# A linear-attention prologue in front of a squared-ReLU feed-forward: one weight load issued earlier, one product on another engine, two input loads swapped

## The chip, the cores and the metric

The kernel runs on one core of one Trainium2 chip. The metric is device time in microseconds (us) of one execution; lower is better. The core has a matrix engine (PE, TensorE), three engines for elementwise work (DVE = VectorE, ACT = ScalarE, POOL = GpSimd), a queue engine (SP, SyncE) that here only issues DMAs, and 16 DMA engines which all queues share. DMAs issued by SP and ACT show in the profile as hardware queues (q1 for SP, q10 for ACT), those issued by POOL as the software queue q0.

## The reference

Two stages, in fp32. The first is a recurrent linear attention over 4 batches, 8 heads, 768 steps and head size 48; the second is a feed-forward layer with a squared ReLU on its output.

```python
for t in range(S):                                            # r, k, v: [B, H, S, D]; w, u: [H, D]
    cur = einsum('bhd,bhe->bhde', u * k[:, :, t], v[:, :, t])
    y[:, :, t] = einsum('bhd,bhde->bhe', r[:, :, t], state + cur)
    state = w[..., None] * state + einsum('bhd,bhe->bhde', k[:, :, t], v[:, :, t])
x = y.transpose(0, 2, 1, 3).reshape(B * S, H * D)             # 3072 x 384
h = maximum(x @ w_in, 0)                                      # w_in: 384 x 2048
out = (h * h) @ w_out                                         # w_out: 2048 x 384
```

## The kernel before, in words

The 768 steps of a batch are cut into 6 chunks of 128, so there are 24 **units** (batch, chunk). Within a unit the recurrence becomes matrix products: keys and receptances are scaled by powers of w (`kh`, `rh`), transposed on PE (`T`, and for the first units `TK`, `TR`), multiplied with each other (`A`), masked (`Bm`), and multiplied with v (`Y`); the state goes from one unit of a batch to the next through a product k·v (`U`, in pairs `UP`) and elementwise updates (`S0`, `ts`, `S`). The term with u is a row sum: `P0` = r·k, `P1` = P0·u, `du` = sum over the head, `dv` = v·du. The result of a unit is copied out of PSUM (`xs`), transposed (`X`, then `xTc`), multiplied with W1 = w_in (`F1`, and `FA` for parts of the first group), passed through ReLU and square (`re`, `sq`), multiplied with W2 = w_out (`F2`), copied (`os`) and stored (`out`).

Units 0 to 3 are handled as two **pairs**: pair 0 is units 0 and 1 (the first two chunks of batch 0), pair 1 is units 2 and 3 (those of batch 1). One load `lp.x.q` brings r, k or v of pair q as 384 KB, in 128 partitions with 8 pieces of 384 bytes each, that is 1024 DMA packets. Later units are loaded one by one (`ld`, 192 KB, pieces of 192 bytes). `Ap.q`, `Bp.q`, `YE.q` / `YD.q`, `YI` and `UP.q` are the pair's forms of A, Bm, Y and U. W1 is loaded in four quarters `V.0` to `V.3` of 512 columns each, W2 in four quarters `W.0` to `W.3`, all by POOL with a cast to bf16; a W1 quarter is 128 partitions with 3 pieces of 1024 bytes, 384 packets. `FA` needs quarter 3, then `F1` of the first group needs quarters 0, 1 and 2. `Z.n` is n tiles of dummy products with the identity.

Nothing is scheduled at run time. A table `ORDER`, read from left to right, gives every step with its engine (A, D, G = POOL, P = PE, S = SP) and, behind the slashes, the buffer or PSUM bank it takes; each engine runs its own steps in this order and waits on semaphores for the others. `UP.1:P/7/3` is the state product of pair 1 on PE into banks 7 and 3. In the trace a step is found by its line: L332 the pair loads, L328 the single loads, L338 V, L341 W, L344 kh, L347 rh, L350 P0, L354 P1, L357 du, L362 dv, L371 TR and TK, L391 Ap, L399 Bp, L456 and L465 YE, L435 and L444 YD, L475 YI, L498 UP, L522 S0, L525 ts, L533 X, L561 FA, L549 F1, L589 F2. Copies by ACT or DVE have the lines of a helper (L257 and L259) and are told apart by their tiles: `rkT` is a copy of transposed keys or receptances (`RC`, `KC`), `vb` the bf16 copy of v, `xs` and `xT` those of the results. In the order's rows the tiles carry numbers: `P_82` belongs to unit 1 and `P_83` to unit 0, `ldv_71` and `ldv_72` hold v of pairs 0 and 1, `ldk_67` and `ldk_68` k of pairs 0 and 1, `W_0` to `W_3` with numbers 183 to 186 are the W1 quarters.

In the table before, the first steps of SP are r.0, k.0, r.1, v.0, k.1, v.1 (pairs 0 and 1) and then single loads of units 4 and 5; POOL makes masks (`mP`, `mJ`), then P0 of unit 1, three W1 quarters, P1 of unit 0, the last W1 quarter and dv of units 1 and 0.

Of the kernel before, what the change touches and what calls it, by code (L numbers as in the profile page):

```python
# [24 lines left out]
ORDER = """
w:A mP.0:G mP.1:G lp.r.0:S/0 lp.k.0:S/0 tab:A lw:A Z.8:P/0 u:A w4:A bw:P/1 lp.r.1:S/1 lp.v.0:S/0 mJ:G lp.k.1:S/1
bu:P/6 Wt.1:A/2 lp.v.1:S/1 Wt.0:A/5 rh.1:D/0 P0.1:G/0 Wk.0:A/4 rh.0:D/1 Wk.1:A/7 ld.r.5:S/4 kh.0:D/1 V.3:G kh.1:D/0
ub:A l4:A TR.0:P/0 P0.0:D/1 V.0:G ld.k.4:S/4 RC.0:A/0 TK.0:P/3 rh.3:D/2 rh.2:D/3 V.1:G P1.1:D du.1:D/1 bc:P/6 TR.1:P/2
KC.0:A/1 ld.r.4:S/5 P1.0:G WLcol:A vb.0:A/0 vb.1:A/1 kh.2:D/3 kh.3:D/2 Z.2:P/5 Ap.0.1:P/0/3 Ap.0.0:P/4/6 V.2:G
TK.1:P/5 ld.k.5:S/5 dv.1:G du.0:D/0 dv.0:G RC.1:A/2 WLm:A Bp.0.1.1:D/0 UP.0:P/7/3 Bp.0.0.1:D/2 YE.0.1:P/2/6  # L30
Bp.0.1.0:D/1 KC.1:A/3 vb.3:A/2 Z.7:P/0 vb.2:A/3 Bp.0.0.0:D/3 YE.0.0:P/2/6 Ap.1.0:P/5/4 P0.2:G/2 S0.0:D ld.v.4:S/4
P1.2:G ts.1:D/1 xs.0:A/0 YI.1:P X.0:P/0 Bp.1.0.1:D/4 UP.1:P/7/3 xs.1:A/1 xTc.0:D/3 Bp.1.0.0:D/6 S0.2:D X.1:P/2
FA.0.0:P/6/4 ts.3:D/0 xTc.1:A/3 FA.0.1:P/6/4 P0.3:G/3 P1.3:G du.2:D/2 F1.0.0:P/5 dv.2:G du.3:D/3 dv.3:G W.2:G Wt.2:A
re.0.6:A/0 re.0.0:A/1 ld.v.5:S/5 Wk.2:A W.1:G rh.5:G/4 W.3:G W.0:G F1.0.1:P/2 Ap.1.1:P/0/6 Bp.1.1.1:D/5 F1.0.2:P/7
re.0.1:A/2 F1.0.3:P/5 re.0.7:A/3 Bp.1.1.0:D/7 YD.1:P/1/2 YI.3:P sq.0.7:A/0 re.0.3:A/4 xs.3:D/2 xs.2:A/3 kh.4:D/5
re.0.2:A/5 ld.k.6:S/6 F1.0.4:P/6 X.2:P/4 X.3:P/2 xTc.3:A/0 sq.0.0:A/2 xTc.2:D/0 sq.0.1:A/1 rh.4:D/5 F1.0.5:P/5
re.0.4:D/3 sq.0.6:A/3 re.0.5:A/2 P0.4:D/4 F1.1.4:P/1 T.4:P/0 Tc.4:D/4 F1.1.7:P/4 sq.0.5:D/4 F1.1.5:P/3 re.1.4:D/1
re.1.7:A/0 ld.r.6:S/6 sq.0.4:A/5 F1.1.1:P/0 re.1.5:D/2 re.1.1:A/3 sq.1.5:D/6 sq.0.3:D/7 F1.1.0:P/6 kh.5:D/4 F1.1.2:P/4
sq.1.1:A/8 F1.1.6:P/5 re.1.2:A/2 re.1.0:D/4 T.5:P/0 re.1.6:D/3 F2.0.2:P/4 F1.1.3:P/6 ld.r.7:S/7 Tc.5:A/5 sq.0.2:D/9
P1.4:D du.4:D/4 A.4:P/5/0 A.5:P/1/2 sq.1.6:A/10 re.1.3:A/5 sq.1.3:A/11 F2.0.1:P/4 sq.1.0:A/12 F2.0.3:P/4 vb.4:G/4  # L40
Bm.4.1:D/0 Bm.4.0:D/1 sq.1.7:A/13 P0.5:D/1 Bm.5.1:D/2 sq.1.4:A/14 F2.1.1:P/5 Bm.5.0:D/3 F2.1.2:P/5 ld.k.7:S/7 dv.4:G
F2.3.2:P/6 Y.4:P/0 P1.5:G sq.1.2:A/15 ld.v.7:S/6 ld.k.9:S/0 xs.4:D/4 du.5:D/0 F2.0.0:P/4 vb.5:A/5 F2.3.0:P/6 Y.5:P/0
dv.5:D xs.5:D/0 P0.6:G/0 P1.6:G ld.v.6:S/7 F2.3.1:P/6 os.0:D/0 ld.r.9:S/0 X.4:P/3 xTc.4:D/1 U.4:P/7 F2.1.0:P/5 X.5:P/0
F2.1.3:P/5 xTc.5:D/1 rh.7:G/6 F1.2.0:P/4 os.1:D/1 S0.4:D F1.2.4:P/0 P0.7:G/2 re.2.0:D/3 out.1:S F1.2.2:P/5 kh.7:D/6
re.2.4:A/5 kh.6:G/0 F1.2.6:P/4 re.2.6:A/4 ld.r.8:S/1 vb.6:A/6 re.2.2:A/0 XB.7:S/6 rh.6:D/0 F1.2.3:P/0 F2.3.3:P/6
kh.9:D/1 re.2.3:A/1 P1.7:D XB.6:S/1 F2.2.2:P/4 du.7:D/1 os.3:D/2 F1.2.1:P/5 S.1:D ld.k.8:S/1 U.5:P/0 S0.5:D dv.7:G
# [9 lines left out]
A.9:P/6/4 A.11:P/1/2 P0.11:D/2 P1.11:G sq.3.2:A/27 F2.6.0:P/3 ld.r.12:S/4 Bm.9.1:D/2 re.3.5:A/3 F2.6.1:P/3 A.8:P/4/0
sq.3.7:A/5 Bm.9.0:D/3 ld.v.12:S/4 dv.9:G sq.3.5:A/7 Bm.11.1:D/5 F1.3.6:P/5 Bm.11.0:D/7 sq.3.4:A/3 du.8:D/4 re.3.6:A/5
F2.7.0:P/2 Bm.8.0:D/0 sq.3.6:A/9 ld.k.12:S/5 ld.r.15:S/7 Y.9:P/1 vb.11:A/2 F2.7.2:P/2 Bm.8.1:D/1 dv.8:D S.9:G
vb.10:A/3 ld.k.14:S/7 F2.6.3:P/3 out.4:A P1.10:G Y.8:P/4 xs.9:D/3 F2.7.3:P/2 A.10:P/5/7 U.10:P/0 xs.8:D/4 P0.13:G/0
kh.13:G/4 X.9:P/6 Bm.10.1:D/4 X.8:P/1 F2.6.2:P/3 xTc.8:A/0 xTc.9:D/0 du.11:D/0 rh.12:G/0 Y.11:P/4 du.10:D/2 dv.10:G  # L60
# [42 lines left out]
re.10.5:D/5 Y.23:P/4 sq.10.5:D/22 F2.19.2:P/6 xs.23:D/3 re.10.3:A/4 sq.10.3:A/23 xX.23:S/1 sq.10.2:A/0 F1.10.6:P/4
F1.10.4:P/0 F2.21.1:P/5 F1.11.1:P/3 out.17:G F1.11.0:P/1 out.16:G re.11.1:D/1 re.11.0:A/0 re.10.1:A/5 sq.11.0:D/27
re.10.4:D/4 F1.11.3:P/2 sq.10.1:D/1 sq.10.4:A/6 re.11.3:D/3 F1.11.2:P/3 sq.11.3:D/3 F2.20.1:P/1 F1.12.1:P/7
re.11.2:A/0 F1.12.2:P/0 F1.12.0:P/2 F2.19.3:P/6 sq.10.0:D/26 re.12.2:D/5 sq.12.2:A/24 re.12.1:D/4 F2.21.2:P/5
sq.11.2:A/25 F1.10.7:P/3 re.10.6:A/3 F2.22.2:P/0 sq.10.6:A/4 re.10.7:D/2 re.12.0:A/5 F2.20.2:P/1 sq.11.1:D/5
sq.10.7:D/10 sq.12.0:A/14 F1.12.3:P/7 sq.12.1:D/18 F2.20.3:P/1 re.12.3:A/0 F2.20.0:P/1 Fh.23.2.0:P/4 os.20:A/5
# [585 lines left out]
```

## Time and profile before

| | |
|---|---|
| times of three runs | 169.10, 171.58, 173.42 us; median 171.58 us |
| profiled execution | 168.49 us, of which its span is 166.8 us |
| busy share of the span | PE 97%, DVE 80%, ACT 62%, POOL 60% |
| DMA moved in the span | 28.02 MB, mean 168 GB/s |
| granted PE clock | full in all 40 slices |

The profiled execution is 3.1 us below the median of the runs and 0.6 us below the lowest. Its span starts with the first instruction; 1.7 us of its time lie outside of it. The page has each engine's busy share; the views on which the prediction draws are the chain of work that ended last (each step followed back to what released it), the timeline by engine (start, duration, engine, line, output<-input, number of instructions merged into the row, and in brackets the idle time before it with its releaser) and the DMA view of a window (packets, MB and busy share by queue; for the DMAs issued in the window their size and the time from issue to landing).

### The profile page before, as it was taken

The page shows a single profiled execution, that of the slowest core. Times are in us where ns is not written, and L with a number is a line of the kernel's source. Part 1 is how long each engine was busy: PE and PEld are TensorE (multiplying, and loading weights), DVE is VectorE, ACT ScalarE, POOL GpSimd, SP SyncE. Part 2 cuts the span into 40 slices and gives each one's busy share as a digit, 9 for nine tenths or more (in the row PEclk, how much of TensorE's full clock was granted, in tenths as well). Part 3 has the DMA queues.
Part 4 walks back from the last instruction along what each step waited for, and adds up shares of the span by engine and source line. Part 5 has one row for each costly group of instructions (what it writes and reads, how often), then busy time and mean ns, then how long its engine had stood idle before and what let it go on. Part 6 is the DMA issues. An engine that isn't in the chain of part 4 may idle for free.

```text
span 166.8 us, 4505 instructions
## 1 busy us (share of the span) xinstructions
...
## 2 busy tenths in 40 slices
...
GB/s 131 324 240 193 201 179 196 196 211 175 157 208 211 176 193 222 171 207 169 216 186 75 221 223 176 216 213 180 193 145 174 192 97 21 120 73 0 2 145 95
DMA packets 97713, 28.02 MB, mean 168 GB/s; under 512 B 92538, under 2 KB 97404, under 8 KB 97692
## 3 DMA queue, kind: packets, MB, share of 16 engines
...
q0 software_dynamic: 3072, 4.33, 13.3%
...
q14 instruction: 7, 0.06, 0.1%
...
## 4 chain that ended last, share of the span: by engine, by line
PE 95%; DMA 2%; ACT 1%; ACTq 0%; issue 0%
PE bank L549 37%; PE bank L589 37%; PE bank L418 4%; PE bank L488 2%; PE bank L371 2%; DMA urow<-in_u_dram 2%; PE bank L486 2%; PE bank L508 2%; PE bank L533 2%; PE bank L603 2%; PE bank L278 1%; PE bank L561 1%; PE bank L391 1%; PE bank L498 1%; PE bank L405 1%; ACT L269 0%
## 5 line engine op out<-in xcount | busy, mean ns | idle before, releaser
L589 PE MATMUL bank<-W,hq 128*128 128x384 bf16 x368 | 68.7, 326 | 0.0
L549 PE MATMUL bank<-xT,W 128*128 128x256 bf16 (+1 forms) x612 | 68.1, 264 | 0.0
L571 ACT ACTIVATE hr<-bank 128x512 bf16<-128x512 f32 x69 | 40.1, 594 | 35.3 <-PE bank L549 33.0
L549 PEld LDWEIGHTS <-W 128*128 128x128 bf16 x612 | 55.0, 98 | 8.4 <-issue 0.6
L589 PEld LDWEIGHTS <-hq 128*128 128x128 bf16 x368 | 33.5, 98 | 18.5
L578 ACT ACTIVATE hq<-hr 128x512 bf16<-128x512 bf16 x72 | 41.9, 625 | 6.0 <-DVE hr L573 5.4
L426 DVE TENSOR_TENSOR Bm<-bank,maskJT 128x512 bf16<-128x512 f32 x40 | 25.5, 681 | 3.7 <-PE bank L418 3.7
L573 DVE TENSOR_SCALAR hr<-bank 128x512 bf16<-128x512 f32 x27 | 18.1, 681 | 5.6 <-PE bank L549 4.0
L354 POOL TENSOR_TENSOR P<-P,ub 128x384 f32<-128x384 f32 x15 | 16.7, 1111 | 6.0 <-DVE P L350 5.4
L362 POOL TENSOR_TENSOR dv<-ldv,du 128x384 f32<-128x384 f32 (+1 forms) x18 | 15.1, 849 | 6.9 <-DVE du L357 4.4
L347 POOL TENSOR_TENSOR rk<-ldr,Wt 128x384 bf16<-128x384 f32 x15 | 15.8, 1056 | 0.0
L350 POOL TENSOR_TENSOR P<-ldr,ldk 128x384 f32<-128x384 f32 x13 | 13.6, 1046 | 3.0 <-DMA ldr<-in_r_dram 1.8
L519 DVE TENSOR_TENSOR xs<-bank,dv 128x384 bf16<-128x384 f32 x20 | 11.0, 552 | 4.4 <-PE bank L488 2.1
L528 POOL TENSOR_TENSOR S0W<-ts,WLm 128x384 bf16<-128x384 f32 x10 | 11.0, 1104 | 4.7 <-DVE ts L525 3.3
L580 DVE TENSOR_TENSOR hq<-hr 128x512 bf16<-128x512 bf16 x24 | 12.9, 550 | 1.2 <-ACT hr L571 0.8
L259 POOL CAST vb<-ldv 128x384 bf16<-128x384 f32 x10 | 5.6, 557 | 13.1 <-DMA ldv<-in_v_dram 13.1
L344 POOL TENSOR_TENSOR rk<-ldk,Wk 128x384 bf16<-128x384 f32 x12 | 12.6, 1056 | 1.2 <-DMA ldk<-in_k_dram 1.2
L357 DVE TENSOR_REDUCE du<-P 128x8 f32<-128x384 f32 x24 | 12.9, 542 | 0.3 <-POOL P L354 0.2
L259 DVE COPY os<-bank 128x384 f32<-128x384 f32 x11 | 6.0, 549 | 6.2 <-PE bank L589 6.1
L525 DVE TENSOR_TENSOR ts<-bank,S0W 128x384 f32<-128x384 f32 x16 | 8.8, 547 | 2.7 <-PE bank L508 2.5
L488 PE MATMUL bank<-vb,Bm 128*128 128x48 bf16 x160 | 9.5, 183 | 0.0
L257 ACT COPY xT<-bank 128x384 bf16<-128x384 bf16 x8 | 3.7, 480 | 8.5 <-PE bank L533 8.5
...
## 6 DMA issues: line engine op xcount, KB each, us to landing
...
W<-in_moe_w_in_dram POOLq DMA_DIRECT2D x4, 384.0 KB, 9.0
W<-in_moe_w_out_dram POOLq DMA_DIRECT2D x4, 384.0 KB, 7.8
...
```

The costliest lines, as they stand in the source:

```text
L347: e.tensor_mul(rk[slot[f"rk{i}"]][:, 0, :, 0:D], loaded("r", i), Do.factor("t", i % 2 if i < PAIRED else 2))
L350: e.tensor_mul(P0b[slot[f"P{i}"]], loaded("r", i), loaded("k", i))
L354: e.tensor_mul(t, t, bank("bu")[:, 0 : H * D].rearrange("p (h d) -> p h d", h=H) if i in EARLY_U else ub)
L357: e.tensor_reduce(dub[slot[f"dv{i}"]], P0b[slot[f"P{i}"]], axis=mybir.AxisListType.X, op=ALU.add)
L362: e.tensor_mul(dv_of(i) if i < PAIRED else dvb[slot[f"dv{i}"]], loaded("v", i), t)
L426: e.tensor_mul(Bmb[slot[f"Bm{i}{h}"]], heads(bank(f"bA{i}{h}"), 128), mask_b)
L549: e.matmul(hp[:, fi, :], W1[f // 4][:, c, 256 * (f // 2 % 2) : 256 * (f // 2 % 2 + 1)].rearrange("p (m j) -> p j m", j=2)[:, f % 2, :], xt ...
L571: e.activation(hr, hp, AF.Relu)
L573: e.tensor_scalar_max(hr, hp, 0.0)
L578: e.activation(hq, hr, AF.Square)
L580: e.tensor_mul(hq, hr, hr)
L589: e.matmul(bank(f"bO{i}")[:, 0:d_model], hqb[slot[f"hq{g},{f // m}"]][:, at : at + L], W2[q][:, f % 4, :], start=(seen[i] == 1 and f % 4 = ...
```

## The change

Only the table `ORDER` differs. Three moves are those of the title; with them a few more steps of the prologue change places, and some later products take other PSUM banks. The core of the difference (the first lines of the table):

```diff
-w:A mP.0:G mP.1:G lp.r.0:S/0 lp.k.0:S/0 tab:A lw:A Z.8:P/0 u:A w4:A bw:P/1 lp.r.1:S/1 lp.v.0:S/0 mJ:G lp.k.1:S/1
-bu:P/6 Wt.1:A/2 lp.v.1:S/1 Wt.0:A/5 rh.1:D/0 P0.1:G/0 Wk.0:A/4 rh.0:D/1 Wk.1:A/7 ld.r.5:S/4 kh.0:D/1 V.3:G kh.1:D/0
-ub:A l4:A TR.0:P/0 P0.0:D/1 V.0:G ld.k.4:S/4 RC.0:A/0 TK.0:P/3 rh.3:D/2 rh.2:D/3 V.1:G P1.1:D du.1:D/1 bc:P/6 TR.1:P/2
-KC.0:A/1 ld.r.4:S/5 P1.0:G WLcol:A vb.0:A/0 vb.1:A/1 kh.2:D/3 kh.3:D/2 Z.2:P/5 Ap.0.1:P/0/3 Ap.0.0:P/4/6 V.2:G
-TK.1:P/5 ld.k.5:S/5 dv.1:G du.0:D/0 dv.0:G RC.1:A/2 WLm:A Bp.0.1.1:D/0 UP.0:P/7/3 Bp.0.0.1:D/2 YE.0.1:P/2/6
-Bp.0.1.0:D/1 KC.1:A/3 vb.3:A/2 Z.7:P/0 vb.2:A/3 Bp.0.0.0:D/3 YE.0.0:P/2/6 Ap.1.0:P/5/4 P0.2:G/2 S0.0:D ld.v.4:S/4
-P1.2:G ts.1:D/1 xs.0:A/0 YI.1:P X.0:P/0 Bp.1.0.1:D/4 UP.1:P/7/3 xs.1:A/1 xTc.0:D/3 Bp.1.0.0:D/6 S0.2:D X.1:P/2
-FA.0.0:P/6/4 ts.3:D/0 xTc.1:A/3 FA.0.1:P/6/4 P0.3:G/3 P1.3:G du.2:D/2 F1.0.0:P/5 dv.2:G du.3:D/3 dv.3:G W.2:G Wt.2:A
+w:A mP.0:G mP.1:G lp.r.0:S/0 lp.k.0:S/0 tab:A lw:A Z.8:P/0 u:A w4:A bw:P/1 lp.r.1:S/1 lp.k.1:S/1 lp.v.0:S/0 mJ:G
+bu:P/6 Wt.1:A/2 lp.v.1:S/1 Wt.0:A/5 rh.1:D/0 V.3:G P0.1:G/0 Wk.0:A/4 rh.0:D/1 Wk.1:A/7 ld.r.5:S/4 kh.0:D/1 kh.1:D/0
+ub:A l4:A TR.0:P/0 P0.0:D/1 V.0:G P1.1:G ld.k.4:S/4 RC.0:A/0 TK.0:P/3 rh.3:D/2 rh.2:D/3 V.1:G du.1:D/1 TR.1:P/2 bc:P/6
+KC.0:A/1 ld.r.4:S/5 P1.0:G WLcol:A RC.1:A/2 vb.0:A/0 vb.1:A/1 kh.2:D/3 kh.3:D/2 Z.2:P/5 Ap.0.1:P/0/3 Ap.0.0:P/4/6
+TK.1:P/5 ld.k.5:S/5 dv.1:G du.0:D/0 dv.0:G V.2:G WLm:A Bp.0.1.1:D/0 UP.0:P/7/3 Bp.0.0.1:D/2 YE.0.1:P/2/6 Bp.0.1.0:D/1
+KC.1:A/3 Z.7:P/0 Bp.0.0.0:D/3 YE.0.0:P/2/6 Ap.1.0:P/5/4 P0.2:G/2 S0.0:D ld.v.4:S/4 P1.2:G ts.1:D/1 xs.0:A/0 YI.1:P
+X.0:P/0 xs.1:A/1 vb.3:A/2 vb.2:A/3 xTc.0:D/3 X.1:P/2 FA.0.0:P/6/7 UP.1:P/3/0 Bp.1.0.1:D/4 Bp.1.0.0:D/6 S0.2:D ts.3:D/0
+xTc.1:A/3 FA.0.1:P/6/7 P0.3:G/3 P1.3:G du.2:D/2 F1.0.0:P/5 dv.2:G du.3:D/3 dv.3:G W.2:G Wt.2:A re.0.6:A/0 re.0.0:A/1
```

On POOL, from the end of the masks to the first products of unit 2 (before with -, changed with +; `W_3_186` is W1's quarter 3, `P_82` unit 1's product):

```order
 L226 AFFINE_SELECT maskJT<-maskJT 128x128
+L338 DMA W_3_186<-in_moe_w_in_dram 128x3x512
 L350 TENSOR_TENSOR P_82<-ldr_63,ldk_67 128x384
-L338 DMA W_3_186<-in_moe_w_in_dram 128x3x512
 L338 DMA W_0_183<-in_moe_w_in_dram 128x3x512
+L354 TENSOR_TENSOR P_82<-P_82,ub 128x384
 L338 DMA W_1_184<-in_moe_w_in_dram 128x3x512
 L354 TENSOR_TENSOR P_83<-P_83,ub 128x384
-L338 DMA W_2_185<-in_moe_w_in_dram 128x3x512
 L362 TENSOR_TENSOR dv_93<-ldv_71,du_88 128x384
 L362 TENSOR_TENSOR dv_92<-ldv_71,du_87 128x384
+L338 DMA W_2_185<-in_moe_w_in_dram 128x3x512
```

Quarter 3 went ahead of unit 1's r·k, unit 1's product with u came in (from DVE, where it stood ahead of `du_88`), and quarter 2 went behind both dv of pair 0.

On ACT, from the copy of pair 0's transposed keys to the copy of the first transposed result (`rkT_107` and `rkT_108` are pair 1's transposed receptances and keys, `vb_97` and `vb_98` v of pair 0, `vb_99` and `vb_100` v of pair 1):

```order
 L316 ACTIVATE wcol<-bank_181 128x4
+L257 COPY rkT_107<-bank_177 128x1024
 L257 CAST vb_97<-ldv_71 128x384
 L257 CAST vb_98<-ldv_71 128x384
-L257 COPY rkT_107<-bank_177 128x1024
 L257 COPY WLm<-wcol 48x4x48 x2
 L257 COPY rkT_108<-bank_180 128x1024
+L257 CAST xs_120<-bank_177 128x384
+L257 CAST xs_121<-bank_181 128x384
 L257 CAST vb_99<-ldv_72 128x384
 L257 CAST vb_100<-ldv_72 128x384
```

The copies of pair 0's v now stand behind one more copy of 1024 columns, and those of pair 1's v behind the two copies of pair 0's results.

On PE, at the first feed-forward products. In the kernel before, the last transposition of unit 0's result (`xs_120`) is followed at once by UP.1 (`L498`):

```order
L533 LDWEIGHTS xs_120
L533 MATMUL bank_175<-identity,xs_120 128x128
L498 LDWEIGHTS rk_78
L498 MATMUL bank_182<-vb_100,rk_78 128x96
L498 LDWEIGHTS rk_78
L498 MATMUL bank_178<-vb_100,rk_78 128x96
```

In the changed one UP.1 stands behind the last product of FA for unit 0, and takes banks 178 and 175 in place of 182 and 178:

```order
L561 LDWEIGHTS W_3_186
L561 MATMUL bank_182<-xT_3_130,W_3_186 128x128
L498 LDWEIGHTS rk_78
L498 MATMUL bank_178<-vb_100,rk_78 128x96
L498 LDWEIGHTS rk_78
L498 MATMUL bank_175<-vb_100,rk_78 128x96
```

Between the two transpositions X.0 and X.1 PE now has nothing in between. On DVE the copy of unit 0's transposed result moved ahead of the first mask product of pair 1, as the table shows (`xTc.0` and `Bp.1.0.1`).

More of the change, by code (lines that the diff above doesn't have):

```diff
@@ L31 @@
-Bp.0.1.0:D/1 KC.1:A/3 vb.3:A/2 Z.7:P/0 vb.2:A/3 Bp.0.0.0:D/3 YE.0.0:P/2/6 Ap.1.0:P/5/4 P0.2:G/2 S0.0:D ld.v.4:S/4
-P1.2:G ts.1:D/1 xs.0:A/0 YI.1:P X.0:P/0 Bp.1.0.1:D/4 UP.1:P/7/3 xs.1:A/1 xTc.0:D/3 Bp.1.0.0:D/6 S0.2:D X.1:P/2
-FA.0.0:P/6/4 ts.3:D/0 xTc.1:A/3 FA.0.1:P/6/4 P0.3:G/3 P1.3:G du.2:D/2 F1.0.0:P/5 dv.2:G du.3:D/3 dv.3:G W.2:G Wt.2:A
-re.0.6:A/0 re.0.0:A/1 ld.v.5:S/5 Wk.2:A W.1:G rh.5:G/4 W.3:G W.0:G F1.0.1:P/2 Ap.1.1:P/0/6 Bp.1.1.1:D/5 F1.0.2:P/7
-re.0.1:A/2 F1.0.3:P/5 re.0.7:A/3 Bp.1.1.0:D/7 YD.1:P/1/2 YI.3:P sq.0.7:A/0 re.0.3:A/4 xs.3:D/2 xs.2:A/3 kh.4:D/5
@@ L36 @@
[L36 to L40, printed above, removed]
@@ L41 @@
-Bm.4.1:D/0 Bm.4.0:D/1 sq.1.7:A/13 P0.5:D/1 Bm.5.1:D/2 sq.1.4:A/14 F2.1.1:P/5 Bm.5.0:D/3 F2.1.2:P/5 ld.k.7:S/7 dv.4:G
-F2.3.2:P/6 Y.4:P/0 P1.5:G sq.1.2:A/15 ld.v.7:S/6 ld.k.9:S/0 xs.4:D/4 du.5:D/0 F2.0.0:P/4 vb.5:A/5 F2.3.0:P/6 Y.5:P/0
-dv.5:D xs.5:D/0 P0.6:G/0 P1.6:G ld.v.6:S/7 F2.3.1:P/6 os.0:D/0 ld.r.9:S/0 X.4:P/3 xTc.4:D/1 U.4:P/7 F2.1.0:P/5 X.5:P/0
+w:A mP.0:G mP.1:G lp.r.0:S/0 lp.k.0:S/0 tab:A lw:A Z.8:P/0 u:A w4:A bw:P/1 lp.r.1:S/1 lp.k.1:S/1 lp.v.0:S/0 mJ:G
+bu:P/6 Wt.1:A/2 lp.v.1:S/1 Wt.0:A/5 rh.1:D/0 V.3:G P0.1:G/0 Wk.0:A/4 rh.0:D/1 Wk.1:A/7 ld.r.5:S/4 kh.0:D/1 kh.1:D/0
@@ new lines @@
+xTc.1:A/3 FA.0.1:P/6/7 P0.3:G/3 P1.3:G du.2:D/2 F1.0.0:P/5 dv.2:G du.3:D/3 dv.3:G W.2:G Wt.2:A re.0.6:A/0 re.0.0:A/1
+ld.v.5:S/5 Wk.2:A W.1:G rh.5:G/4 W.3:G W.0:G F1.0.1:P/2 Ap.1.1:P/0/6 Bp.1.1.1:D/5 F1.0.2:P/4 re.0.1:A/2 F1.0.3:P/5
+re.0.7:A/3 Bp.1.1.0:D/7 YD.1:P/1/2 YI.3:P sq.0.7:A/0 re.0.3:A/4 xs.3:D/2 xs.2:A/3 kh.4:D/5 re.0.2:A/5 ld.k.6:S/6
+F1.0.4:P/6 X.2:P/3 X.3:P/2 xTc.3:A/0 sq.0.0:A/2 xTc.2:D/0 sq.0.1:A/1 rh.4:D/5 F1.0.5:P/5 re.0.4:D/3 sq.0.6:A/3
+re.0.5:A/2 P0.4:D/4 F1.1.4:P/1 T.4:P/0 Tc.4:D/4 F1.1.7:P/4 sq.0.5:D/4 F1.1.5:P/3 re.1.4:D/1 re.1.7:A/0 ld.r.6:S/6
@@ new lines @@
+sq.0.4:A/5 F1.1.1:P/0 re.1.5:D/2 re.1.1:A/3 sq.1.5:D/6 sq.0.3:D/7 F1.1.0:P/6 kh.5:D/4 F1.1.2:P/4 sq.1.1:A/8 F1.1.6:P/5
+re.1.2:A/2 re.1.0:D/4 T.5:P/0 re.1.6:D/3 F2.0.2:P/4 F1.1.3:P/6 ld.r.7:S/7 Tc.5:A/5 sq.0.2:D/9 P1.4:D du.4:D/4
+A.4:P/5/0 A.5:P/1/2 sq.1.6:A/10 re.1.3:A/5 sq.1.3:A/11 F2.0.1:P/4 sq.1.0:A/12 F2.0.3:P/4 vb.4:G/4 Bm.4.1:D/0
+Bm.4.0:D/1 sq.1.7:A/13 P0.5:D/1 Bm.5.1:D/2 sq.1.4:A/14 F2.1.1:P/5 Bm.5.0:D/3 F2.1.2:P/5 ld.k.7:S/7 dv.4:G F2.3.2:P/6
+Y.4:P/0 P1.5:G sq.1.2:A/15 ld.v.7:S/6 ld.k.9:S/0 xs.4:D/4 du.5:D/0 F2.0.0:P/4 vb.5:A/5 F2.3.0:P/6 Y.5:P/0 dv.5:D
@@ L44 @@
+xs.5:D/0 P0.6:G/0 P1.6:G ld.v.6:S/7 F2.3.1:P/6 os.0:D/0 ld.r.9:S/0 X.4:P/3 xTc.4:D/1 U.4:P/7 F2.1.0:P/5 X.5:P/0
 F2.1.3:P/5 xTc.5:D/1 rh.7:G/6 F1.2.0:P/4 os.1:D/1 S0.4:D F1.2.4:P/0 P0.7:G/2 re.2.0:D/3 out.1:S F1.2.2:P/5 kh.7:D/6
```

26 lines of the change are left out of this document (13 added, 13 removed).

## The prediction

> **What bounds the kernel now.** I read the page first, then the chain of work that ended last, then the early rows of each engine, then the DMA view of short windows. The page's part on the chain:
>
> ```profile
> PE 95%; DMA 2%; ACT 1%; ACTq 0%; issue 0%
> ```
>
> PE is the path almost everywhere, so an early edit counts only by what it does to the start of PE's long run. That start, piece by piece (start, us, what):
>
> ```profile
> 2.12 3.25 DMA urow<-in_u_dram
> ...
> 5.42 1.64 PE bank L278 x2
> ...
> 8.88 0.52 PE bank L313 x2
> 9.40 0.96 PE bank L371 x8
> ...
> 12.54 0.75 PE bank L498 x13
> ...
> 13.55 0.49 PE bank L621 x4
> ...
> 14.35 0.34 PE bank L465 x4
> 14.69 0.48 ACT xs L257
> ...
> 15.21 0.34 PE bank L533 x3
> 15.55 0.45 PE bank L498 x16
> 16.00 0.27 PE bank L533 x3
> 16.27 1.40 PE bank L561 x24
> ...
> 19.33 1.42 PE bank L549 x12
> 20.74 0.29 PE bank L435 x4
> ```
>
> PE waits for the load of u until 5.42 and then hardly at all. The whole prologue up to FA (L561) at 16.27 is one gapless queue, with 0.49 us of dummy products (L621) in it. So nothing that makes DVE or a load earlier shortens PE's run: the most that can be gained is the sum of the small gaps between these rows, a few tenths of a us. What can move the end is a wait that opens in this queue, or a change of PE's own order.
>
> **The DMA queues decide whether a wait opens.** Moving the W1 quarter puts it among the pair loads. POOL's rows and SP's rows now:
>
> ```profile
> 4.08 0.29 POOL L226 TENSOR_SCALAR_AFFINE_SELECT maskJT<-maskJT 128x128 bf16<-128x128 bf16 x1
> 5.62 0.99 POOL L350 TENSOR_TENSOR P<-ldr,ldk 128x384 f32<-128x384 f32 x1 [1.24 <-DMA ldk<-in_k_dram]
> 6.55 2.49 POOL L338 DMA_DIRECT2D W<-in_moe_w_in_dram  x3
> 9.07 1.28 POOL L354 TENSOR_TENSOR P<-P,ub 128x384 f32<-128x384 f32 x1
> 10.30 0.80 POOL L338 DMA_DIRECT2D W<-in_moe_w_in_dram  x1
> ```
>
> ```profile
> 3.04 1.23 SPq L332 DMA_DIRECT2D ldv<-in_v_dram  x1
> 4.31 1.33 SPq L332 DMA_DIRECT2D ldk<-in_k_dram  x1
> 5.68 1.15 SPq L332 DMA_DIRECT2D ldv<-in_v_dram  x1
> 6.88 1.15 SPq L328 DMA_DIRECT2D ldr<-in_r_dram  x1
> ```
>
> V.3's issue took 6.55 to about 7.4; it will take about 4.4 to 5.2. What moved on the 16 engines, by queue (packets, MB, share), in the windows 2.4 to 4.7, 8 to 9.5, 10.6 to 11.4 and 13 to 19 us:
>
> ```profile
> q1 hardware_dynamic: 1770, 0.67, 108.2%
> ...
> q1 hardware_dynamic: 1185, 0.45, 110.8%
> ...
> q0 software_dynamic: 162, 0.17, 124.8%
> ...
> q0 software_dynamic: 959, 0.95, 93.2%
> q1 hardware_dynamic: 957, 0.18, 27.7%
> ```
>
> From 8 to 9.5 V.3 had been issued, but only pair loads moved (q1; no row of q0). From 10.6 to 11.4 only V.3 moved, although SP had issued the next load (6.88, ended 8.03). And the load of u, 1.5 KB, issued by 2.35, did not move at all between 2.4 and 4.7: no row of its queue q10. I read this as a line in the order of arrival: what has been issued waits behind everything whose issue had ended before, and goes ahead of what ended later. Only when both queues have a long backlog (13 to 19) do they take turns, packet by packet.
>
> By this reading V.3 (issue over at 5.2) will stand behind r.0, k.0, r.1 and the now earlier k.1 (over at 4.27) and ahead of v.0 (over at 5.64). Its 384 packets at 162 in 0.8 us cost 1.9 us. The landings, from the DMA view for the issue at 4.31 and from the view of line L338 by windows (us from issue to landing, for V.3, for V.0 with V.1, for V.2):
>
> ```profile
> ldk<-in_k_dram SPq DMA_DIRECT2D x1, 384.0 KB, 5.0
> ```
>
> ```profile
> DMA to landing us min/median/max: 6.3/6.3/6.3
> ...
> DMA to landing us min/median/max: 7.7/9.0/10.3
> ...
> DMA to landing us min/median/max: 10.6/10.6/10.6
> ```
>
> The fifth pair load lands at 4.31 + 5.0 = 9.3 now; v.0, the new fifth, lands at 9.3 + 1.9 = 11.2. Who needs it: ACT's copies of v.
>
> ```profile
> 8.06 1.93 ACT L257 COPY rkT<-bank 128x1024 bf16<-128x1024 bf16 x2 [0.31 <-PE bank L371]
> ...
> 9.94 0.94 ACT L257 CAST vb<-ldv 128x384 bf16<-128x384 f32 x2
> 10.76 1.03 ACT L257 COPY rkT<-bank 128x1024 bf16<-128x1024 bf16 x1
> ```
>
> **Part by part.**
>
> *ACT and UP.0.* The copies `vb` now come behind `wcol`, which needs bc, now behind TR.1 on PE. TR.1 can start when TK.0 ends, at 8.9, so bc ends at 8.9 + 0.96 + 0.52 = 10.4; `wcol` (0.2) and then RC.1 (1.03) run to 11.6 or 11.7; `vb` to 11.7 + 0.94 = 12.6. v.0 at 11.2 is half a us early. UP.0 starts at 12.65 in place of 12.54: **+0.1 us**.
>
> *P1 of unit 1.* DVE loses 0.71 us, POOL gains 1.0 to 1.28 us (its P1 row).
>
> ```profile
> 8.78 0.71 DVE L354 TENSOR_TENSOR P<-P,ub 128x384 f32<-128x384 f32 x1
> ...
> 11.39 2.47 DVE L399 TENSOR_TENSOR Bm<-bank,maskP 128x512 bf16<-128x512 f32 x4
> ```
>
> DVE's mask products Bp start at 11.39 because du of unit 0 stands ahead of them, and du waits for POOL's P1 of unit 0, which still ends at about 10.4 (V.1 now about 8.7 to 9.4, then 1.0). Bp can start at about 11.1, but YE.0.0, which needs the last of them (13.86 now), comes on PE behind the dummy products, at 14.04, anyway: **0**. If that cover were gone it would be a gain of 0.2 us. On POOL both dv of pair 0 now end at about 11.4 + 1.6 = 13.0 (two take 1.62 in a row below), still ahead of their use on PE (L465, 14.35): 0. V.2's issue slips from 10.30 to about 13.0, but V.1 is then still moving, so its data lose nothing.
>
> *UP.1 behind FA.0.0.* This is the one edit on PE itself. Now UP.1 (0.45 us) fills the time from X.0's end at 15.55 to X.1 at 16.00, while DVE copies X.0's result. Moved, it leaves a hole: X.1 runs in it (0.27 to 0.34, as soon as ACT's second `xs` is there, about 15.7), FA.0.0 starts when DVE has copied X.0's result, about 16.05 in place of 16.27, and UP.1's 0.45 comes later: 0.45 - 0.22 = **+0.2 us** at FA's end. Bounds: +0.45 if the copy starts no earlier, -0.1 if it ends 0.3 us sooner, since DVE is free there.
>
> *Behind UP.1.* S0, ts and du of pair 1 wait for it and slip by 0.7 to 0.8 us, and with them dv of pair 1 and the W2 loads on POOL:
>
> ```profile
> 18.21 1.62 POOL L362 TENSOR_TENSOR dv<-ldv,du 128x384 bf16<-128x384 f32 x2 [1.39 <-DVE du L357]
> 19.77 1.48 POOL L341 DMA_DIRECT2D W<-in_moe_w_out_dram  x2
> ```
>
> dv ends at 19.83 + 0.75 = 20.6; PE takes it at 20.74 + 0.3 (L435). Cover left: 0.4 us. Beyond that, each 0.1 us is a stall of 0.1 us; I take 0, with +0.5 as the far end.
>
> *v of pair 1.* It stands behind v.0, and its end takes turns with V.0. A pair load takes 1.3 us alone (1024 packets at 1185 in 1.5 us); in turns for half of it, at 160 packets per us, 3.8 us. So it lands 1.3 to 3.8 us behind v.0, at 12.5 to 15.0. ACT copies it behind both `xs`, at about 15.6: 0.
>
> **The sum**: 0.1 + 0.2 = +0.3 us, carried to the end because PE has no slack behind. Against the profiled execution: 168.49 + 0.3 = 168.8 us. The runs have a median 3.1 us above that execution, so I forecast 171.58 + 0.3 = **171.9 us** for a median of runs. From the bounds of the terms: -0.3 to +1.2. The runs spread over 4.3 us, so about 2% (3.4 us) is what a measurement of this kernel can tell from no change.
>
> **Rivals.**
>
> *The queues take turns from the first packet.* Then V.3 and the quarters behind it slow the pair loads from its first packet on, as in the window 13 to 19, where q1 moved 957 packets in 6 us, 160 per us. V.3's first packets came no sooner than 9.5, 3.0 us after its issue began: say 7.4 us now. v.0 then takes 6.4 us in place of 1.3 and lands at 9.3 + 5.1 = 14.4; `vb` ends at 15.4, and UP.0 waits for it from 12.54 on: +2.8 us. If V.3 starts sooner, at 6.3 (halfway between its issue's end and 7.4), k.1 is hit as well: the four quarters keep q0 busy for 1536 / 160 = 9.6 us, to 15.9, by when k.1 and half of v.0 are through; the rest takes 0.7 us and lands near 17, UP.0 waits to 18: +5.5 us. So 171.3 to 174.0 by the profiled execution, 174.4 to 177.1 by the median. For it: the window 13 to 19. Against: 8 to 9.5 and 10.6 to 11.4, where both queues had work and only one moved. It decides from v.0 landing later than 11.7. The Trainium skill, "DMA: Bandwidth & Descriptors", Queues, rings and completion order, says that each DMA engine goes round robin between the queues it has work for, a packet at a time. By that rule this rival would be the forecast; the trace agrees from 11.4 us on and disagrees before, and the measured windows decide for me.
>
> *The W1 quarters set the time of the slower runs.* V.1 lands at 8.3 + 10.3 = 18.6 and is used at 19.33; V.2 at 20.9 and is used at about 21.7. Covers of 0.7 us can be gone in a run that is 3 us longer than the profiled one. Moved up, V.3's whole 1.9 us lies ahead, and both quarters land at least 1 us earlier. If that wait is what the longer runs have, the median falls by 1 to 3 us, to 169 to 170.6; past the 2% only if the runs come down to the profiled execution. For it: the spread of the runs. Against: the chain of the profiled execution shows no such wait, and nothing shows what the longer runs waited for.
>
> *It moves nothing on the DMA side.* V.3 waits behind all six pair loads as now, landing at 12.9. Then only PE's order counts: +0.2 to +0.3, 171.9 as well.
>
> **How the numbers follow.** Forecast with small terms 0.70, turns 0.13, W1 quarters in slower runs 0.11, nothing on the DMA side 0.06. Two thirds of the turns rival and a little noise lie above 2%: 0.11; a third of the W1 rival and noise lie below: 0.07; within 2%: 0.82. The range goes from 168.7 (the W1 rival's gain of 3, less noise) to 174.9 (past the near end of turns).
>
> **What would show it.** Right: in the changed profile UP.0 (L498) at about 12.6; a window of about 7.5 to 9.3 with only q0 moving; v.0 landing near 11.2; FA (L561) at about 16.1, broken by L498, ending near 18.0; dv of pair 1 ending near 20.6; the span 0.3 us longer. Wrong: an idle time of PE before L498 with the load of v as releaser (turns), or before L435 with POOL (dv late), or runs whose spread shrinks to below 2 us (W1 quarters).

## The result, and the profile after

The change makes the kernel slower. Twenty runs of each: 169.94 us in the median before (169.10 to 173.42), 172.25 us changed (169.80 to 175.05), a ratio of 1.0096, interval 1.0067 to 1.0125, that is +1.6 us. A second set of runs (after_2 below) gave 169.60 and 173.83 us, 1.0225 (1.0171 to 1.0279), that is +3.8 us. These ratios compare only runs within 1.5% of each kernel's fastest, which leaves out 8 of the 20 runs of the changed kernel; between all runs the medians differ by 2.3 us in the first set and 4.2 us in the second. The profiled execution has a span of 168.8 us, 2.0 more than before.

The page's part on the chain, which had PE with 95% before:

```profile
PE 80%; DMA 11%; SPq 4%; DVE 2%; issue 1%; ACT 1%; POOL 0%
```

A load is on the path now. The chain between 4 and 24 us (start, us, what) names it:

```profile
5.49 11.56 DMA ldv<-in_v_dram
17.05 0.02 issue
17.07 0.94 ACT vb L257 x2
18.01 0.04 issue
18.05 0.52 PE bank L498 x16
18.57 0.78 PE bank L561 x12
19.34 1.31 PE bank L549 x12
```

The DMA issued behind 5.45 is v of pair 1. It lands at 17.05; ACT makes its bf16 copy; UP.1 (L498) starts at 18.05, and FA's second half and F1 follow. Before, the first F1 (L549) stood at 17.67 in the chain, now at 19.34: 1.67 of the 2.0 us are lost here. PE's own rows, first before, then changed:

```profile
12.47 0.82 PE L498 MATMUL bank<-vb,rk 64*128 64x96 bf16 x16
...
13.48 0.56 PE L621 MATMUL bank<-identity 128*128 128x512 bf16 x4
...
15.21 0.34 PE L533 MATMUL bank<-identity,xs 128*128 128x128 bf16 x3
...
17.51 1.47 PE L549 MATMUL bank<-xT,W 128*128 128x256 bf16 x12
```

```profile
12.71 0.82 PE L498 MATMUL bank<-vb,rk 64*128 64x96 bf16 x16
...
13.78 0.93 PE L621 MATMUL bank<-identity 128*128 128x512 bf16 x4
...
16.15 0.83 PE L533 MATMUL bank<-identity,xs 128*128 128x128 bf16 x6
16.94 0.83 PE L561 MATMUL bank<-xT,W 128*128 128x128 bf16 x12
18.05 0.52 PE L498 MATMUL bank<-vb,rk 64*128 64x96 bf16 x16 [0.28 <-ACT vb L257]
...
19.18 1.47 PE L549 MATMUL bank<-xT,W 128*128 128x256 bf16 x12
```

UP.0 (12.71) is within 0.1 us of its forecast, and 0.24 us behind its row of before. Behind it the dummy products (L621) take 0.93 us against 0.56, and X.0 (L533) starts 0.94 us later than before: PE works at a slower pace there until 15.4, where the trace's record of PE's clock has the step to full speed (13.3 in the profile of before). FA.0.0 runs at 16.94, and then PE waits 0.28 us for ACT's copy. So two delays lie beside each other up to UP.1: PE alone, at its slower pace and in its new order, would have come there at 17.77, and the load does not let it start before 18.05. In this profile, then, the 1.67 us are 0.24 up to UP.0, 0.70 of pace from there to X.0, about 0.4 of PE's new order (up1_only below) and 0.28 of wait for the load.

The DMA side, by queue in the windows 7.5 to 8, 8 to 9.5, 10 to 10.5 and 12 to 13 us (packets, MB, share):

```profile
q0 software_dynamic: 98, 0.10, 121.1%
q1 hardware_dynamic: 14, 0.00, 3.4%
...
q0 software_dynamic: 224, 0.23, 93.7%
q1 hardware_dynamic: 186, 0.07, 26.4%
...
q1 hardware_dynamic: 412, 0.16, 113.8%
q0 software_dynamic: 5, 0.00, 1.6%
...
q0 software_dynamic: 146, 0.15, 87.6%
q1 hardware_dynamic: 147, 0.06, 32.2%
```

V.3 (q0) comes behind the fourth pair load and has the engines nearly to itself until 8. From 8 to 9.5 the fifth, v of pair 0 (q1), moves beside it, 186 packets against 224, and then goes alone at 412 packets per half us. From about 11.5 us on V.0 and v of pair 1 move in equal numbers, about 147 packets per us each.

### The profile page after: what moved, and what is told of

It is laid out like the page before. It is cut to its first block, busy times and chain, and to the rows that moved or that the text cites. A ratio compares the mean times of both kernels' runs of the same rounds, so it can differ in the third digit from the quotient of the medians.

```text
span 168.8 us, 4501 instructions
## 1 busy us (share of the span) xinstructions
PE 162.5 (96%) x1772; PEld 121.4 (72%) x1772; DVE 131.4 (78%) x250; ACT 103.8 (61%) x196; POOL 101.0 (60%) x125
## 4 chain that ended last, share of the span: by engine, by line
PE 80%; DMA 11%; SPq 4%; DVE 2%; issue 1%; ACT 1%; POOL 0%
PE bank L549 34%; PE bank L589 33%; DMA ldv<-in_v_dram 9%; PE bank L418 3%; SPq L332 3%; PE bank L488 2%; DMA rkT<-rk 2%; PE bank L486 2%; PE bank L603 2%; PE bank L508 1%; DVE Bm L426 1%; PE bank L533 1%; SPq L411 1%; ACT vb L257 1%; PE bank L405 1%
## 5 line engine op out<-in xcount | busy, mean ns | idle before, releaser
L549 PE MATMUL bank<-xT,W 128*128 128x256 bf16 (+1 forms) x612 | 68.2, 264 | 0.0
L549 PEld LDWEIGHTS <-W 128*128 128x128 bf16 x612 | 54.9, 98 | 8.4 <-issue 0.4
L344 POOL TENSOR_TENSOR rk<-ldk,Wk 128x384 bf16<-128x384 f32 x12 | 12.9, 1080 | 2.2 <-DMA ldk<-in_k_dram 2.1
L580 DVE TENSOR_TENSOR hq<-hr 128x512 bf16<-128x512 bf16 x24 | 12.2, 520 | 1.1 <-ACT hr L571 0.8
L488 PEld LDWEIGHTS <-Bm 128*128 128x128 bf16 x160 | 8.3, 96 | 1.4 <-DVE Bm L426 0.4
L257 ACT COPY os<-bank 128x384 f32<-128x384 f32 (+2 forms) x14 | 6.3, 458 | 4.3 <-PE bank L589 2.3
```

Source lines behind the costliest of these rows:

```text
L344: e.tensor_mul(rk[slot[f"rk{i}"]][:, 1, :, 0:D], loaded("k", i), Do.factor("k", i % 2 if i < PAIRED else 2))
L488: e.matmul(y[:, hc, D * h : D * (h + 1)], m[h][:, hc, :], vb[:, 2 * hc + h, :], start=(c == 0), stop=True, skip_group_check=True,)
L549: e.matmul(hp[:, fi, :], W1[f // 4][:, c, 256 * (f // 2 % 2) : 256 * (f // 2 % 2 + 1)].rearrange("p (m j) -> p j m", j=2)[:, f % 2, :], xt ...
```

## Experiments

Theory 1: v of pair 1 is late because it stands behind V.3 and then beside V.0 and V.1. Theory 2: the loss is PE's new order and its slower pace, not the load. Theory 3, that PE's step to full pace is set by how early it is kept busy, came up later, with before_warm. Each ratio below is to the kernel before in the same set (medians 169.68, 169.51 and 169.60 us).

**v3_back.** The changed kernel, V.3 behind P0 of unit 1 again:

```diff
-rh.1:D/0 V.3:G P0.1:G/0
+rh.1:D/0 P0.1:G/0 V.3:G
```

> The changed kernel with V.3 behind P0.1 on POOL again, all else kept. Theory 1 (loads move in the order of arrival; V.3 ahead of v.0 makes v.0 late by 1.9 us and puts v.1 into turns with the other W1 quarters, so that UP.1 waits for v.1): v.1 lands near 11 us in place of 17.05, PE has no idle time ahead of UP.1, about 0.4 us of the changed kernel's loss goes: about +0.9 us against before where the changed one has +1.6. Theory 2 (only PE's new order and a later step of PE to full speed cost time; the loads do not matter): as the changed kernel, +1.6 us.

171.06 us, 1.0074 (1.0035 to 1.0114). ACT copied v of pair 1 at 15.88 with no wait, UP.1 stood at 16.97, the first F1 at 18.10 instead of 19.18. The interval, +0.6 to +1.9 us, holds the figures of both theories; the trace speaks for the first, though part of the gain at F1 is that PE stepped to its full pace at 9.9 us here.

**v0_later.** The changed kernel, V.3 early as it is, V.0 and V.1 each behind one of POOL's P1:

```diff
-P0.0:D/1 V.0:G P1.1:G ld.k.4:S/4
+P0.0:D/1 P1.1:G V.0:G ld.k.4:S/4
...
-rh.3:D/2 rh.2:D/3 V.1:G du.1:D/1
+rh.3:D/2 rh.2:D/3 du.1:D/1
...
-P1.0:G WLcol:A
+P1.0:G V.1:G WLcol:A
```

> The changed kernel with V.0 behind P1 of unit 1 and V.1 behind P1 of unit 0 on POOL; V.3 stays early. Theory 1: v.1 has the queue for itself behind v.0 and lands near 12.5, UP.1 waits for nothing, the W1 quarters still come in time: about 0.4 us less than the changed kernel, +1.2 us against before. Theory 2: as the changed kernel, +1.6 us.

171.10 us, 1.0055 (1.0012 to 1.0098). The queues from 10 to 11.5 us, ACT's copy of v of pair 1, and UP.1:

```profile
q1 hardware_dynamic: 1282, 0.49, 116.6%
q0 software_dynamic: 2, 0.00, 0.8%
```

```profile
15.41 0.93 ACT L257 CAST vb<-ldv 128x384 bf16<-128x384 f32 x2
```

```profile
16.50 0.51 PE L498 MATMUL bank<-vb,rk 64*128 64x96 bf16 x16
```

With V.0's issue starting at 8.76 and not at 6.56, only the pair loads move in that window, but for two packets. V of pair 1 was through by 12.00 on the last of its DMA engines (the trace's completion records), against 16.66 in the changed kernel; its copy waits for nothing but ACT's own order. So it is sharing with V.0 and V.1 that makes v of pair 1 late. UP.1 comes 1.55 us earlier, which is not all the load: PE stepped to full pace at 10.4 us in this execution.

**up1_back.** The changed kernel up to `KC.1`, then the table of before (UP.1 between X.0 and X.1, the copies of v of pair 1 ahead of `xs`):

```diff
-KC.1:A/3 Z.7:P/0
+KC.1:A/3 vb.3:A/2 Z.7:P/0 vb.2:A/3
...
-X.0:P/0 xs.1:A/1 vb.3:A/2 vb.2:A/3 xTc.0:D/3 X.1:P/2 FA.0.0:P/6/7 UP.1:P/3/0 Bp.1.0.1:D/4
+X.0:P/0 Bp.1.0.1:D/4 UP.1:P/7/3 xs.1:A/1 xTc.0:D/3
```

> The changed kernel up to KC.1, and the order of before from there: UP.1 between X.0 and X.1, the copies of pair 1's v ahead of both xs on ACT; V.3 stays early. Theory 1: the copies of v wait on ACT for v.1 until about 17 us, xs of unit 0 stands behind them, and X.0 comes at about 18 in place of 15.2: +2.5 to +3.5 us against before. Theory 2: PE's order is that of before, so +0.2 to +0.3 us is left, or +0.9 if the step to full speed comes late again.

173.67 us, 1.023 (1.0161 to 1.0299). Theory 2's order falls here: with PE's new order taken back the loss against before is 3.9 us (2.7 to 5.1), where theory 2 gave it 0.2 to 0.9. ACT:

```profile
12.83 0.93 ACT L257 CAST vb<-ldv 128x384 bf16<-128x384 f32 x2 [1.24 <-DMA ldv<-in_v_dram]
...
17.48 0.93 ACT L257 CAST vb<-ldv 128x384 bf16<-128x384 f32 x2 [2.08 <-DMA ldv<-in_v_dram]
18.32 0.85 ACT L257 CAST xs<-bank 128x384 bf16<-128x384 f32 x2
```

The copy of v of pair 1 now waits 2.08 us and holds up both `xs`; X.0 starts at 18.84, against 16.15 in the changed kernel's first profile. That putting UP.1 later, as the change does, softens the late load is what these rows suggest; the times do not show it, since the changed kernel lost 1.6 us in its first set and 3.8 in its second. The first row was not expected: v of pair 0 was late too, by 1.3 us against the changed kernel's first profile.

**kv_back.** The changed kernel with v of pair 0 ahead of k of pair 1 again:

```diff
-lp.r.1:S/1 lp.k.1:S/1 lp.v.0:S/0
+lp.r.1:S/1 lp.v.0:S/0 lp.k.1:S/1
```

> The changed kernel with v of pair 0 loaded ahead of k of pair 1 again; V.3 stays early. Theory 1: now k.1 stands behind V.3 and lands near 11.2 in place of 8; kh of units 2 and 3 start near 11.3 in place of 9.4, the mask products behind them on DVE start near 12.9 in place of 11.5, TK.1 and YE.0.0 wait on PE: +0.7 to +1.2 us more than the changed kernel, +2.3 to +2.8 us against before. If the queues took turns packet by packet from the start, k.1 would be later still (13 or more) and the loss over 4 us. Theory 2: as the changed kernel, +1.6 us.

173.81 us, 1.022 (1.0157 to 1.0282), that is +3.7 us. UP.0 at 13.27, ACT's copy of v of pair 1 at 17.66, the first F1 at 21.37. The fifth load is k of pair 1 now, and DVE's `kh` (L344) waits 1.72 us for it. UP.0 stands 0.56 us later than in the changed kernel's first profile, so the swap helps there; in the whole time that is not shown, since the changed kernel's second set lost 3.8 us too. Of the 3.7 us a part is pace again, which stayed at the slower step until 21.3.

**p1_swap.** The kernel before with P1 of unit 1 on POOL and the two loads swapped:

```diff
-lp.r.1:S/1 lp.v.0:S/0 mJ:G lp.k.1:S/1
+lp.r.1:S/1 lp.k.1:S/1 lp.v.0:S/0 mJ:G
...
-V.1:G P1.1:D du.1:D/1
+P1.1:G V.1:G du.1:D/1
```

> The kernel before with two of the three named edits: P1 of unit 1 on POOL ahead of V.1, and k of pair 1 loaded ahead of v of pair 0. V.3 stays where it was. Theory 1: v.0 lands at about 9.3 in place of 8.1, still ahead of its copy on ACT at 9.9, and POOL's extra 1.0 us delays only the issue of V.1 and V.2, whose data queue anyway: 0 us against before, within 0.3. If DVE's shorter queue were worth its 0.7 us: -0.7.

170.06 us, 1.0025 (1.0001 to 1.0050): at most 0.8 us. The first F1 starts at 17.46, where a second profile of before (below) has it; what it costs lies later and was not found.

**up1_only.** The kernel before up to `Bp.0.1.0`, then the changed table:

```diff
-KC.1:A/3 vb.3:A/2 Z.7:P/0 vb.2:A/3
+KC.1:A/3 Z.7:P/0
...
-X.0:P/0 Bp.1.0.1:D/4 UP.1:P/7/3 xs.1:A/1 xTc.0:D/3
+X.0:P/0 xs.1:A/1 vb.3:A/2 vb.2:A/3 xTc.0:D/3 X.1:P/2 FA.0.0:P/6/7 UP.1:P/3/0 Bp.1.0.1:D/4
```

> The kernel before up to the mask product Bp.0.1.0, then the changed order: UP.1 behind FA.0.0, copies of pair 1's v behind both xs on ACT. V.3, P1 and the loads as before, so v.1 is there in time. Theory 1: only the hole between X.0 and FA.0.0 costs: +0.2 to +0.5 us against before. If the later step of PE to full speed comes from this order, +1 us or more.

170.17 us, 1.0029 (0.9998 to 1.0060): +0.5 us by its middle. X.1 stood at 15.67 behind a wait of 0.15 us, UP.1 at 16.72, the first F1 at 17.85, 0.39 behind p1_swap, which has before's order there.

**before_warm and after_warm.** Four more tiles of dummy products in PE's wait for u, in the kernel before and in the changed one:

```diff
-bw:P/1 lp.r.1:S/1
+bw:P/1 Z.4:P/0 lp.r.1:S/1
```

> The kernel before with one more dummy product of 512 columns on PE in its wait for the load of u (4.9 to 5.4 us), which delays nothing. Theory 3 (PE goes to full speed at the end of the first stretch of a few us in which it was busy enough; where those stretches lie differs from run to run, and a wait in the prologue can miss one): the step comes sooner on the mean, -0.2 to -1 us and a smaller spread of the runs. Without theory 3: 0.

> The changed kernel with the same dummy product. Theory 3: the changed kernel's loss beyond the waits for v.1 and the hole (about 0.8 us) is the later step, so it falls from +1.6 to about +0.8 us against before, and the spread of its runs (169.8 to 175.1) shrinks. Without theory 3: as the changed kernel, +1.6 us.

169.92 us, 1.0010 (0.9979 to 1.0041), and 171.29 us, 1.0108 (1.0061 to 1.0155). The dummies do nothing to the time that could be told, so theory 3 in this form found no support: the step to full pace came at 14.97 and, by the durations of the rows, at about 14.7 us. In after_warm X.0 was 0.26 us earlier than in the changed kernel's profile and UP.1 still stood at 18.04, behind a longer wait for ACT's copy (0.53): the load pins it.

**after_2 and before_2.** Both kernels again as they are:

> The changed kernel once more, for a second profile and beside the next two. Theory 1 in its present form (v.1 lands near 17 us because it takes turns with W1 quarters, and it alone sets UP.1 at about 18.0, whether PE is at full speed by 13 or by 15 us): UP.1 again at about 18.0 and F1 of the first group at about 19.2, +1.6 us against before. If PE's step to full speed set it, both would move with the step.

> The kernel before once more, for a second profile. If the later part of the program (behind the first F1) has a time of its own that differs from run to run, its length differs by some tenths of a us up to 1.5 from the 149.3 us of the first profile, as it does among the profiles of the experiments; no theory of the change speaks of it.

The changed one ran at 173.83 us, 1.0225 (1.0171 to 1.0279), with a span of 172.0; before's profile has 167.4, a difference of 4.6 us. UP.1 stood at 20.01 and not at 18.0, so this expectation missed. Behind the first F1 the changed kernel takes 149.7 and 150.0 us in its two profiles, the one before 149.3 and 149.9, so nearly all of the difference lies ahead of F1. From the chain of after_2, and PE's rows there:

```profile
4.32 8.72 DMA ldv<-in_v_dram
...
13.48 0.52 ACT vb L257
```

```profile
13.63 0.26 PE L498 MATMUL bank<-vb,rk 64*128 64x96 bf16 x2 [0.86 <-ACT vb L257]
14.04 0.74 PE L498 MATMUL bank<-vb,rk 64*128 64x96 bf16 x14
...
15.03 0.93 PE L621 MATMUL bank<-identity 128*128 128x512 bf16 x4
...
18.59 1.49 PE L561 MATMUL bank<-xT,W 128*128 128x128 bf16 x12
20.01 0.82 PE L498 MATMUL bank<-vb,rk 64*128 64x96 bf16 x16
20.76 1.46 PE L561 MATMUL bank<-xT,W 128*128 128x128 bf16 x12
22.02 1.80 PE L549 MATMUL bank<-xT,W 128*128 128x256 bf16 x12
```

This time it is v of pair 0 (issue behind 4.28) that lands late, at 13.04; most of UP.0 starts at 14.04. The trace has a completion record of each DMA engine for a load: here 15 of the 16 were through with v of pair 0 between 10.34 and 10.89 us, and one at 12.73. In the first profile all 16 ended between 10.5 and 11.09; in up1_back the last came at 12.49. ACT's copy waits for the last one. My reading is that an engine on which a rest of v of pair 0 is left when V.0 begins sends that rest in turns; the trace does not say which engine a packet went through, so this is not shown. Compare PE in before_2:

```profile
12.13 0.50 PE L498 MATMUL bank<-vb,rk 64*128 64x96 bf16 x15 [0.26 <-DVE Bm L399]
...
13.32 0.54 PE L621 MATMUL bank<-identity 128*128 128x512 bf16 x4 [0.22 <-DVE Bm L399]
...
15.44 0.51 PE L498 MATMUL bank<-vb,rk 64*128 64x96 bf16 x16
...
16.06 1.56 PE L561 MATMUL bank<-xT,W 128*128 128x128 bf16 x24
17.46 1.47 PE L549 MATMUL bank<-xT,W 128*128 128x256 bf16 x12
```

UP.0's main row starts 1.9 us earlier here, the first F1 4.6 us earlier. The other 2.7 us are mostly pace: the 24 FA products take 1.56 us here and 1.49 + 1.46 there, UP.1 0.51 and 0.82, the dummies 0.54 and 0.93. So in this execution the late load stands beside two losses, the wait and a longer stretch at PE's slower pace; that the wait brings the longer stretch is not shown.

**v0_later_up1_back.** Both earlier edits together: V.3 early, V.0 and V.1 later, UP.1 and the copies in before's places:

```diff
-P0.0:D/1 V.0:G P1.1:G ld.k.4:S/4
+P0.0:D/1 P1.1:G V.0:G ld.k.4:S/4
...
-KC.1:A/3 Z.7:P/0
+KC.1:A/3 vb.3:A/2 Z.7:P/0 vb.2:A/3
```

> The changed kernel with V.0 and V.1 issued later (behind P1 of units 1 and 0) and with UP.1 and the copies of v in the places of before; V.3 stays early, k.1 ahead of v.0. Theory 1: v.1 is there by about 13, neither the hole nor the wait is left; +0.1 to +0.5 us against before, from bc and the copies of v of pair 0 alone. If V.3 early costs anything by itself, +1 us or more.

170.15 us, 1.0038 (1.0007 to 1.0070). ACT copied v of pair 1 at 14.08 with no wait; the step to full pace came at 16.6, and the first F1 at 18.73. An early V.3 does no harm by itself that could be told from the 1.0025 of p1_swap; the harm needs V.0 and V.1 right behind it. This kernel and up1_back differ in nothing but the places of V.0 and V.1 on POOL, and their ratios, 1.0038 and 1.0230, have intervals that lie apart: with before's order on PE the two places are worth about 3.3 us, slower pace included.

**v3_only.** The kernel before with V.3 early and nothing else (the other W1 quarters move up behind it):

```diff
-rh.1:D/0 P0.1:G/0 Wk.0:A/4 rh.0:D/1 Wk.1:A/7 ld.r.5:S/4 kh.0:D/1 V.3:G
+rh.1:D/0 V.3:G P0.1:G/0 Wk.0:A/4 rh.0:D/1 Wk.1:A/7 ld.r.5:S/4 kh.0:D/1
```

> The kernel before with V.3 issued right behind the masks and nothing else. Theory 1: V.3 goes ahead of k.1, which lands near 11.2; kh of units 2 and 3 and the mask products behind them are late by 1.2 to 1.5 us; v.1 takes turns with the quarters, and the copies of v.1 hold xs of unit 0 on ACT: +3 to +5 us against before. Theory 2 (loads do not matter): 0.

176.74 us, 1.0358 (1.0289 to 1.0428): +6.1 us on four runs, more than theory 1 gave it. Two waits in its rows of PE and ACT:

```profile
12.36 0.64 PE L391 MATMUL bank<-rkT,rkT 48*64 48x128 bf16 x16 [1.30 <-DVE rk L344]
```

```profile
17.51 0.93 ACT L257 CAST vb<-ldv 128x384 bf16<-128x384 f32 x2 [2.49 <-DMA ldv<-in_v_dram]
```

DVE's `kh` (L344) had waited for k of pair 1, the fifth load here; v of pair 1 is about as late as in the changed kernel (ACT's copy starts at 17.51 and at 17.07), and here that copy stands ahead of `xs`. That is the title's first part alone, and the dearest kernel of all. With the other parts of the change the loss was 1.6 us in one set and 3.8 in the other, so they take back a part of it, 2.3 to 4.5 us by these figures.

## Why the prediction was right, and where it was wrong

The forecast of 171.9 us lies 0.35 below the median, and a change of less than 2% is what the first set shows (the second, 1.0225, leaves that open). But the difference is not right: I forecast +0.3 us, and it is +1.6 in the first set and +3.8 in the second. The number is near by luck: it stood on a median of three runs, 171.58, which twenty runs put at 169.94. The bounds of my terms add up to -0.2 and +1.05 us, not to the -0.3 and +1.2 that I wrote, and the +1.6 us lies above both.

- *Order on the DMA queues*: half right. V.3 began as forecast, at 7.16, as k of pair 1 ended. But the window from 7.5 to 9.3 was to show q0 only, and it did so only until about 8: from 8 to 9.5 v of pair 0 moved 186 packets beside 224 of V.3, and no engine was through with V.3 before 9.06. So it took turns with V.3 and did not wait behind it. V of pair 0 was to land at 11.2 and was taken by POOL at 11.54; that came out all the same, because v of pair 0 has the more packets left and ends last whether the two loads take turns or not, so the landing does not prove the order. The rival of queues that take turns had priced v of pair 0 beside V.0 as well, and V.0 did not move before 10.90. The cover of "half a us" depends on the slowest of 16 engines; in after_2 it was gone, and most of UP.0 started at 14.04. There that rival is partly true, at about half of its price of 2.8 us.
- *v of pair 1*: the step that failed. I let it land "at 12.5 to 15.0", with half of its packets in turns at 160 per us, and wrote 0. It landed at 17.05. By the trace's packets about 630 of its 1024 moved after 11.5, in turns with V.0 and V.1 and at 147 per us, and its 16 engines were through between 15.04 and 16.66, where I had one time for all. By my own reading, that a load goes ahead of what was issued after it, it should not have taken turns at all: v of pair 1 had its issue over at 6.70 (4.27 + 2.43), V.0 at 7.37 (6.56 + 0.81). So the reading was wrong here too. The round robin by packets of the Trainium skill ("DMA: Bandwidth & Descriptors", Queues, rings and completion order), which I set behind the windows, is what these two loads did from about 11.5 on: 146 and 147 packets in 12 to 13 us, where a packet of the Trainium skill is a group of descriptors and the profile's rows count single pieces of 384 and 1024 bytes. The price, by kernels that differ only in V.0 and V.1: 3.3 us with before's order on PE (up1_back and v0_later_up1_back). In the changed order it is 1.0055 with them later and 1.0096 and 1.0225 as they are, so 0.7 us in one set, where the intervals overlap, and 2.9 in the other. In the first profile the wait itself is 0.28 us; in after_warm, with PE 0.26 us earlier, UP.1 stood where it was. Of the loss in the second set's profile a large part is the other load, v of pair 0, and the slower pace.
- *PE's pace*: a term that the sum did not have. It is 0.70 of the 1.67 us in the first profile and most of 2.7 us in after_2. Since the step to full pace differs between executions of one kernel, how much of it the change brings stays open.
- *ACT and UP.0*, +0.1: forecast 12.65, measured 12.71 in the first profile.
- *UP.1 behind FA.0.0*, +0.2, bounds -0.1 to +0.45: up1_only has +0.39 at the first F1. Within the bounds. FA as a whole was to run from 16.1 to 18.0 and ran from 16.94 to 19.34, for the reasons above.
- *P1 of unit 1*, 0: p1_swap, which has the swap too, shows 0 at the first F1 and +0.4 us (0 to 0.8) in the whole.
- *Behind UP.1*: dv of pair 1 was to end at 20.6, with 0.4 us of cover. The row below shows it ending at 21.96, 1.4 us later than forecast, with UP.1; PE took it at 22.42 (L435), so it cost nothing more.

```profile
20.34 1.62 POOL L362 TENSOR_TENSOR dv<-ldv,du 128x384 bf16<-128x384 f32 x2 [2.31 <-DVE du L357]
```

- *The W1 quarters in slower runs*: wrong. The spread was to shrink below 2 us; it grew from 4.3 to 5.25.

What I named as proof of a wrong forecast was a wait before L498 with the load of v behind it. That wait is there: in the first profile at UP.1 (0.28 us) and not at UP.0, in after_2 at UP.0 (0.86 us).

What stays open: what sets the moment of V.3's first packet. It came 2.98, 2.84 and 3.01 us after the start of its issue in before, in the changed kernel and in v3_back. V.0's came 2.65 us after in v0_later and 3.48 in v0_later_up1_back. Each of these five came just as a load of SP's queue ended on the first of the engines. In the changed kernel V.0's came 4.34 us after, 0.4 us behind the first engine's end of v of pair 0. A place in the order of arrival gives the five times, but not the 4.34 us, nor the two loads that took turns against it, v of pair 0 with V.3 and v of pair 1 with V.0. A delay of about 2.7 us that ends at the next load's boundary gives the five times within 0.1 us and allows the turns, but not the 0.4 us. No run tested either by itself. Also open is what p1_swap loses behind the first F1, and why the changed kernel lost 1.6 us by the ratio in one set and 3.8 in the other; the late engine in v of pair 0 was seen in one of the two profiles of its table, and in up1_back, whose table is the same up to there.
